# Layer 0's kept K page: first of its block instead of last, with the scores in a rotating PSUM bank

## The chip, the cores and the metric

The kernel runs on one core of one Trainium2 chip. The metric is the device time of one execution in microseconds (us). Three runs of the kernel before took 545.01 us in the median, 544.82 to 545.41. The profile shown is one more execution, taken with the hardware profiler.

## What is computed

A decode step with two layers, each of attention over a sliding window and of a gated feed-forward part. There is one query token of 640 numbers. Attention has 32 heads of 192 numbers, every head has its own K and V, and only the last 4096 positions of the cache are used. Both layers use the same weights and the same K and V caches:

```python
def _A_ref(x, k_cache, v_cache, wq, wo):
    ...
    k = jnp.repeat(k_cache[:, :, Sk - W:, :], rep, axis=1)      # W = 4096, rep = 1
    v = jnp.repeat(v_cache[:, :, Sk - W:, :], rep, axis=1)
    scores = jnp.einsum("bhqd,bhkd->bhqk", q, k) * (Dh ** -0.5)
    p = _softmax(scores, axis=-1)
    o = jnp.einsum("bhqk,bhkd->bhqd", p, v)
    ...

x = A_x
x = x + _A_ref(_layernorm(x, axis=-1), A_k_cache, A_v_cache, A_wq, A_wo)
x = x + _B_ref(_layernorm(x, axis=-1), B_w1, B_w3, B_w2)
x = x + _A_ref(_layernorm(x, axis=-1), A_k_cache, A_v_cache, A_wq, A_wo)
x = x + _B_ref(_layernorm(x, axis=-1), B_w1, B_w3, B_w2)
```

The layers must follow each other, but a K page read from memory for layer 0 can be used in layer 1 again if it stays on the chip.

## The kernel before

**Pages and slots.** Everything large is loaded in pages of 128 partitions x 6144 bf16 elements, 1536 KB: one page is the window of one head's K, or of its V, or a piece of a weight matrix. SBUF has an arena of 16 slots, one page each (`NSLOT`, L29). `loads` (L151-178) is the list of all pages in the order in which they are fetched. `refill` (L180) takes the head of that list whenever a slot is free and issues its DMA from the SP queue (L187); `done` (L203) gives a slot back and calls `refill`. This runs while the program is built, so which load takes which slot is fixed. On the chip, the load waits until the last reader of the slot's old page is over, and SP issues the loads strictly in the order of the list: a load whose slot is not free yet holds back those behind it.

**The loop.** `attention` (L429) goes over `i` from 0 to 41. Step `i` handles V page number `i - 10` (`LEAD`, L33) if there is one, and then K page number `i` if there is one. In this document K0 to K31 and V0 to V31 are these numbers, not head numbers. Heads come in blocks of eight (`HB`); `ORDER` (L146) gives the order of the blocks, 3, 2, 1, 0 in layer 0 and 1, 0, 2, 3 in layer 1. So K24 to K31 of layer 0 are heads 0 to 7. V0 to V7 belong to the first block, V24 to V31 to the last, and a block's V pages follow its K pages by ten steps. The loads stand in the same order: V(i - 10), K(i), V(i - 9), K(i + 1) and so on.

**A K page** (`k_page`, L272) is transposed in place by DVE in two halves (L281), then 12 matmuls on PE add the scores of its head into a PSUM bank that the eight heads of the block share. **The softmax of a block** (`softmax_head`, L294) runs after the eighth: a maximum over the bank, small transposes, the exponential on ACT (L310), one more transpose (L313). `softmax_place` (L316), two steps later, copies the probabilities into the tile `ptm` (five copies on ACT and three on DVE, L323) and takes the row sums with a matmul into `rl_ps` and a reciprocal (L327). **A V page** (`v_page`, L330) is 16 matmuls with `ptm` into the bank `o_ps` of its block; then its slot is given back. **`combine`** (L345) takes a finished block's o: ACT copies it out of PSUM (L347), two matmuls with `sel` bring it into `ot_ps`, and DVE scales and sums it (L353, L356). `rl_ps` and `ot_ps` are turns of the same single buffer in PSUM. In a block's first V step, the V page is done first and then the `combine` of the block before it (L440-444); the last block's `combine` stands after the loop (L462).

**What is kept for layer 1.** The K pages of 14 heads (`RETAIN`, L31) are not loaded again in layer 1. Thirteen of them simply keep their slot, already transposed. The fourteenth, head 7 (`STASH`, L30), gives its slot back: `stash` (L191) copies its page from SBUF to PSUM, five banks of 512 x 4 bytes a partition into the tile `pss`, and the rest of the page to the SBUF tile `rest` (L195, L198, all on DVE). In layer 1, in the place of head 7's load, the page is copied back into a free slot (L189). The closer layer 0 comes to its end, the more slots are held by kept pages; at its end three slots are left for all other pages.

**PSUM.** `pss` is five banks of the eight. In layer 0 the scores of block 0, 1, 2 and 3 use its banks 0, 1, 0 and 1 (L452). In layer 1 the first two blocks' scores come from the pool `ps_a` (L450), since `pss` still holds the kept page. `ps_a` is two banks in rotation, used by q, by the o of each block and by the projections. `ps_m` is one bank for small things.

So head 7, K31, is the last K page of layer 0, while its block's scores are in bank 1 of `pss`: `k_page` saves four banks and the rest (L290), then the softmax reads the scores, and the last bank is saved after it (L457); then the slot is given back (L458).

All instructions shown are kept in program order on their engine (`pin`, L70).

Of the kernel before, what the change touches and what calls it, by code (L numbers as in the profile page):

```python
# [18 lines left out]
H = 32  # L19
# [3 lines left out]
HB = 8  # L23
NB = H // HB
PGW = 6144
# [4 lines left out]
STASH = 7  # L30
RETAIN = (0, 1, 2, 3, 4, 5, 6, 7, 8, 11, 14, 18, 21, 24)  # L31
NSTASH = 5120
# [4 lines left out]
def _ap(t, p0, npart, off, dims):  # L37
    ps = t.ap[0][0]
    return bass.AP(t.tensor, t.offset + p0 * ps + off, [[ps, npart]] + [list(d) for d in dims])
# [3 lines left out]
def kernel(  # L43
# [13 lines left out]
    nc = tc.nc  # L57
# [12 lines left out]
    def pin(ins):  # L70
        tc.keep_in_program_order(ins)
        return ins

    def mm(*a, **k):
        return pin(nc.tensor.matmul(*a, **k))  # L75
# [57 lines left out]
    arena = arn.tile([P, NSLOT * PGW], BF16, name="arena")  # L133
# [14 lines left out]
    def head(layer, g):  # L148
        return HB * ORDER[layer][g // HB] + g % HB

    for layer in range(2):  # L151
        for c in range(NCH):
            loads.append((("q", layer, c), [(0, PGW, wq_v[c])]))
        for i in range(H + LEAD):
            for kind, g, cache in (("v", i - LEAD, A_v_cache), ("k", i, A_k_cache)):
                if not 0 <= g < H:
                    continue
                h = head(layer, g)
                if kind == "k" and layer == 1 and h in RETAIN:
                    if h == STASH:  # L160
                        loads.append((("k", 1, h), []))
                    continue
                loads.append(((kind, layer, h),
                              [(0, PGW, cache[0, h, S0:SK, :].rearrange("(p t) d -> p (t d)", p=P))]))
        for w in range(6):
            parts, ci, end = [], 9 * w, min(9 * w + 9, 48)
            while ci < end:
                to = min(end, ci - ci % 12 + 12)
                parts.append((640 * (ci - 9 * w), 640 * (to - ci),
                              wo_v[ORDER[layer][ci // 12]][:, 640 * (ci % 12):640 * (ci % 12 + to - ci)]))  # L170
                ci = to
            loads.append((("o", layer, w), parts))
        loads.append((("fa", layer), [(0, PGW, w1_v[:, 0:PGW])]))
        loads.append((("fb", layer), [(0, PGW, w3_v[:, 0:PGW])]))
        loads.append((("fc", layer), [(0, 1536, w1_v[:, PGW:]), (1536, 1536, w3_v[:, PGW:]),
                                      (3072, 2560, w2_v[:, 0:2560])]))
        loads.append((("fd", layer), [(0, 3840, w2_v[:, 2560:6400]), (3840, 640, w2_v[:, 6400:7040])]
                      + [(None, 640, w2_v[:, 7040:7680])] * (layer == 0)))

    def refill():  # L180
        while free and loads:
            key, parts = loads.pop(0)
            s = free.pop(0)
            home[key] = s
            for off, n, src in parts:
                dst = arena[:, s * PGW + off:s * PGW + off + n] if off is not None else keep[:]
                pin(nc.sync.dma_start(out=dst, in_=src))  # L187
            if not parts:
                stash(arena[:, s * PGW:s * PGW + PGW], False, range(5), True)  # L189

    def stash(x, save, banks, tail):  # L191
        xu, pu, ru = x.bitcast(U32), pss[:].bitcast(U32), rest[:].bitcast(U32)
        for k in banks:
            a, p = xu[:, 512 * k:512 * k + 512], pu[:, 512 * k:512 * k + 512]
            pin(nc.vector.tensor_copy(out=p if save else a, in_=a if save else p))  # L195
        if tail:
            a = xu[:, NSTASH // 2:PGW // 2]
            pin(nc.vector.tensor_copy(out=ru if save else a, in_=a if save else ru))  # L198

    def page(key):  # L200
        return arena[:, home[key] * PGW:home[key] * PGW + PGW]

    def done(key):  # L203
        free.append(home.pop(key))
        refill()
# [57 lines left out]
    def build_w(b):  # L263
        for a in range(4):
            dst = _ap(wst[:], 32 * a, 32, 8 * a + 7, [[382, 4], [191, 2], [32, 6]])
            src = _ap(qt_sb[:], 32 * a, 32, 4 * b, [[1, 4], [96, 2], [16, 6]])
            if a % 2 == 1:
                pin(nc.scalar.copy(out=dst, in_=src))  # L268
            else:
                pin(nc.gpsimd.tensor_copy(out=dst, in_=src))  # L270

    def k_page(layer, g, s_ps):  # L272
        h = head(layer, g)
        hl = h % HB
        fresh = layer == 0 or h not in RETAIN
        key = ("k", layer if fresh or h == STASH else 0, h)
        x = page(key)
        if fresh:
            w = PGW // KSPLIT
            for sp in range(KSPLIT):  # L280
                pin(nc.vector.transpose(x[:, w * sp:w * (sp + 1)].bitcast(U32), x[:, w * sp:w * (sp + 1)].bitcast(U32)))  # L281
        for it in range(6):
            be, par = divmod(it, 2)
            for th in range(2):
                mm(s_ps[32 * th:32 * th + 32, :], lhsT=wst[:, hl, it, :],
                   rhs=_ap(x, 0, P, 3072 * th + 64 * be + par, [[192, 16], [2, 32]]),
                   start=(hl == 0 and it == 0), stop=(hl == HB - 1 and it == 5),
                   tile_position=(0, 32 * th))
        if layer == 0 and h == STASH:
            stash(x, True, (0, 2, 3, 4), True)  # L290
        elif layer == 1 or h not in RETAIN:
            done(key)

# [51 lines left out]
    def combine(pos, o_ps, rl):  # L345
        o_sb = w20
        pin(nc.scalar.copy(out=o_sb[:, 0:384], in_=o_ps[:, 0:384]))  # L347
        ot_ps = ps_m.tile([P, 16, 12], F32, tag="m", name="ot_ps")
        for par in range(2):
            mm(ot_ps[:].rearrange("p q e -> p (q e)"), lhsT=sel[:, par, :, :].rearrange("p h q -> p (h q)"),  # L350
               rhs=o_sb[:, 192 * par:192 * par + 192], start=(par == 0), stop=(par == 1))
        om = w20[:, 384:576].rearrange("p (q e) -> p q e", q=16)
        pin(nc.vector.scalar_tensor_tensor(out=om, in0=ot_ps[:], scalar=rl[:], in1=mask[:].unsqueeze(2).broadcast_to([P, 16, 12]),  # L353
                                           op0=ALU.mult, op1=ALU.mult))
        with nc.allow_low_precision("one nonzero term in each sum"):
            pin(nc.vector.reduce_sum(out=otd[:, 12 * pos:12 * pos + 12], in_=om.rearrange("p q e -> p e q"),  # L356
                                     axis=AX.X))
# [71 lines left out]
    def attention(layer):  # L429
        layernorm()  # L430
        if layer == 0:
            flat = _ap(wst[:], 0, P, 0, [[1, wst[:].free_size()]])
            pin(nc.vector.memset(flat.bitcast(U32), 0))
        qproj(layer)
        s_ps, o_ps, soft, rl = {}, {}, {}, {}
        for i in range(H + LEAD):
            if i >= LEAD:
                g = i - LEAD
                b = g // HB
                if g % HB == 0:  # L440
                    o_ps[b] = ps_a.tile([P, 512], F32, tag="a", name="o_ps")
                v_page(layer, g, o_ps[b])
                if g % HB == 0 and b:
                    combine(b - 1, o_ps.pop(b - 1), rl.pop(b - 1))
            if i < H:
                b = i // HB
                if i % HB == 0:
                    build_w(ORDER[layer][b])
                    if layer == 1 and b < 2:
                        s_ps[b] = ps_a.tile([P, 512], F32, tag="a", name="s_ps")  # L450
                    else:
                        s_ps[b] = pss[:, 512 * (b % 2):512 * (b % 2) + 512]  # L452
                k_page(layer, i, s_ps[b])
                if i % HB == HB - 1:
                    soft[b] = softmax_head(b, s_ps.pop(b))
                    if layer == 0 and i == H - 1:
                        stash(page(("k", 0, STASH)), True, (1,), False)  # L457
                        done(("k", 0, STASH))  # L458
            if (i + 1 - LEAD) % HB == 0 and 0 <= (i + 1 - LEAD) < H:
                b = (i + 1 - LEAD) // HB  # L460
                rl[b] = softmax_place(b, *soft.pop(b))
        combine(NB - 1, o_ps.pop(NB - 1), rl.pop(NB - 1))  # L462
        wo_proj(layer)

    refill()
    ob = cst.tile([P, NCH], BF16, name="ob")
    for layer in range(2):
# [34 lines left out]
```

## Time and profile before

| | us |
|---|---|
| median of three runs | 545.01 |
| the profiled execution | 543.21 |
| its span, first to last instruction | 541.3 |
| PE busy | 286.6 (53%) |
| DVE busy | 225.7 (42%) |
| ACT busy | 41.9 (8%) |
| memory read | 222.40 MB, 411 GB/s over the span |

How to read it: the span is what the profiler saw, the time around it is 1.9 us. "Busy" is the time in which an engine has an instruction of its own in hand; PE's share includes matmuls that overlap. The page's second part cuts the span into 40 equal slices of 13.5 us and gives for each the busy tenths of the engines, the granted TensorE clock and the rate of the DMA. The chain of waits follows the work that ended last backwards from the end. Groups of instructions carry the line of the kernel; all matmuls carry L75, that of a helper, and are told apart by their tiles: `pss` and `s_ps` are scores, `o_ps` is V, `ot_ps` and `rl_ps` are the small ones of `combine` and `softmax_place`. A window lists busy time of each engine, the granted clock, the DMA share and the rate in one stretch. Where a line ends in brackets, they hold the engine's idle time before it and what ended it.

### The profile page before, as it was taken

The page shows a single profiled execution, that of the slowest core. Times are in us where ns is not written, and L with a number is a line of the kernel's source. Part 1 is how long each engine was busy: PE and PEld are TensorE (multiplying, and loading weights), DVE is VectorE, ACT ScalarE, POOL GpSimd, SP SyncE. Part 2 cuts the span into 40 slices and gives each one's busy share as a digit, 9 for nine tenths or more (in the row PEclk, how much of TensorE's full clock was granted, in tenths as well). Part 3 has the DMA queues.
Part 4 walks back from the last instruction along what each step waited for, and adds up shares of the span by engine and source line. Part 5 has one row for each costly group of instructions (what it writes and reads, how often), then busy time and mean ns, then how long its engine had stood idle before and what let it go on. Part 6 is the DMA issues. An engine that isn't in the chain of part 4 may idle for free.

```text
span 541.3 us, 5693 instructions
## 1 busy us (share of the span) xinstructions
PE 286.6 (53%) x2400; PEld 117.6 (22%) x2400; DVE 225.7 (42%) x271; ACT 41.9 (8%) x107; POOL 14.6 (3%) x52
## 2 busy tenths in 40 slices
PE   2355375555663655614445437684555655553544
PEld 1111132222221222201112212241222222221221
DVE  1189755575446654430001119516435644530011
ACT  1100200020001100020000000202000300020000
POOL 5100000000000000000000000000000000000000
PEclk9999765667567757755555658897886677565557
DMA  8999999999999999769999999999999999999995
GB/s 355 425 433 429 428 430 426 433 430 427 431 426 431 431 427 431 306 243 431 423 424 395 419 431 390 425 430 430 428 430 428 429 431 430 429 428 429 426 427 205
DMA packets 22633, 222.77 MB, mean 412 GB/s; under 512 B 2768, under 2 KB 3152, under 8 KB 5456
## 3 DMA queue, kind: packets, MB, share of 16 engines
q1 hardware_dynamic: 22464, 222.41, 97.2%
q8 instruction: 19, 0.31, 0.2%
q14 instruction: 6, 0.05, 0.0%
q10 hardware_dynamic: 144, 0.00, 0.0%
HBM read 222.40 MB, written 0.00 MB: 411 GB/s over the span
## 4 chain that ended last, share of the span: by engine, by line
DMA 78%; PE 11%; DVE 7%; issue 2%; ACT 1%; SPq 0%; POOL 0%; DVEq 0%; ACTq 0%; POOLq 0%
DMA arena<-in_A_k_cache_dram 49%; DMA arena<-in_A_v_cache_dram 10%; DMA arena<-in_A_wo_dram 7%; DMA arena<-in_A_wq_dram 7%; DMA arena<-in_B_w_dram 5%; DVE arena L281 4%; PE pss L75 3%; PE s_ps L75 3%; PE o_ps L75 3%; PE y_ps L75 1%; DVE pss L195 1%; PE q_ps L75 1%; PE u_ps L75 0%; SPq L187 0%; ACT w L310 0%
## 5 line engine op out<-in xcount | busy, mean ns | idle before, releaser
L281 DVE STREAM_TRANSPOSE arena<-arena 128x1536 uint32<-128x1536 uint32 x100 | 171.5, 1755 | 101.2 <-DMA arena<-in_A_k_cache_dram 97.1
L75 PE MATMUL pss<-arena,wst 128*32 128x512 bf16 x576 | 133.2, 545 | 133.7 <-DVE arena L281 131.0
L75 PE MATMUL o_ps<-arena,ptm 128*16 128x384 bf16 (+1 forms) x1024 | 126.5, 459 | 41.2 <-DMA arena<-in_A_v_cache_dram 38.1
L75 PEld LDWEIGHTS <-wst 128*32 128x32 bf16 x768 | 54.1, 114 | 235.5 <-issue 195.0
L75 PEld LDWEIGHTS <-ptm 128*16 128x16 bf16 (+2 forms) x1036 | 47.4, 106 | 82.7 <-issue 69.3
L75 PE MATMUL s_ps<-arena,wst 128*32 128x512 bf16 x192 | 27.5, 426 | 9.2 <-ACT wst L268 4.0
L353 DVE SCALAR_TENSOR_TENSOR w<-ot_ps,rl,mask 128x192 bf16<-128x192 f32 x8 | 3.3, 418 | 63.5 <-PE ot_ps L75 63.5
L75 PE MATMUL y_ps<-arena,otd 128*1 128x320 bf16 x192 | 17.2, 458 | 15.8 <-DMA arena<-in_A_wo_dram 15.8
L305 ACT ACTIVATE tb<-m 32x32 f32<-32x32 f32 x8 | 1.8, 228 | 301.6 <-DVE m L302 301.6
L75 PE MATMUL q_ps<-arena,xs 128*32 128x384 bf16 x160 | 14.5, 519 | 18.4 <-DMA arena<-in_A_wq_dram 15.8
L323 ACT COPY ptm<-w 32x128 bf16<-32x128 bf16 x40 | 16.1, 404 | 26.4 <-PE o_ps L75 24.1
L226 DVE CAST w<-y_ps 128x320 bf16<-128x320 f32 x4 | 2.0, 492 | 37.2 <-PE y_ps L75 37.2
L75 PEld LDWEIGHTS <-xs 128*32 128x32 bf16 x240 | 9.2, 125 | 37.2 <-issue 28.3
L251 DVE CAST ptm<-q_ps 128x768 bf16<-128x768 f32 x2 | 1.9, 958 | 31.4 <-ACT w L249 31.4
L270 POOL COPY wst<-qt_sb 32x48 bf16<-32x48 bf16 x16 | 6.2, 386 | 231.7 <-PE pss L75 190.8
L75 PEld LDWEIGHTS <-otd 128*1 128x1 bf16 x192 | 6.5, 102 | 26.4 <-issue 22.2
L295 DVE TENSOR_REDUCE t<-pss 64x1 f32<-64x512 f32 x6 | 4.1, 682 | 12.4 <-PE pss L75 12.4
L313 DVE STREAM_TRANSPOSE w<-w 64x512 bf16<-64x512 bf16 x8 | 5.6, 705 | 7.2 <-ACT w L310 7.2
L347 ACT CAST w<-o_ps 128x384 bf16<-128x384 f32 x8 | 3.8, 480 | 58.5 <-PE o_ps L75 57.0
L75 PE MATMUL st_ps<-xsq,onesD 128*128 128x12 f32 x8 | 2.3, 367 | 9.2 <-DVE xsq L208 9.2
L295 DVE TENSOR_REDUCE t<-s_ps 64x1 f32<-64x512 f32 x2 | 1.4, 684 | 13.5 <-PE s_ps L75 13.5
L268 ACT COPY wst<-qt_sb 32x48 bf16<-32x48 bf16 x16 | 6.4, 398 | 4.3 <-DVE qt_sb L259 3.9
(78 smaller groups left out, 97.0 us busy)
## 6 DMA issues: line engine op xcount, KB each, us to landing
arena<-in_A_v_cache_dram SPq DMA_DIRECT2D x64, 1536.0 KB, 29.2
arena<-in_A_k_cache_dram SPq DMA_DIRECT2D x50, 1536.0 KB, 29.2
arena<-in_A_wq_dram SPq DMA_DIRECT2D x10, 1536.0 KB, 10.2
arena<-in_A_wo_dram SPq DMA_DIRECT2D x6, 1440.0 KB, 15.7
arena<-in_B_w_dram SPq DMA_DIRECT2D x4, 1536.0 KB, 13.7
arena<-in_A_wo_dram SPq DMA_DIRECT2D x4, 960.0 KB, 16.8
arena<-in_A_wo_dram SPq DMA_DIRECT2D x6, 480.0 KB, 14.2
arena<-in_B_w_dram SPq DMA_DIRECT2D x2, 960.0 KB, 13.3
```

Source lines behind the costliest of these rows:

```text
L75: return pin(nc.tensor.matmul(*a, **k))
L195: pin(nc.vector.tensor_copy(out=p if save else a, in_=a if save else p))
L226: pin(nc.vector.tensor_copy(out=y_sb[:, 320:640], in_=y_ps[1][:, 0:320]))
L251: pin(nc.vector.tensor_copy(out=q_rep[par][:], in_=src))
L268: pin(nc.scalar.copy(out=dst, in_=src))
L270: pin(nc.gpsimd.tensor_copy(out=dst, in_=src))
L281: pin(nc.vector.transpose(x[:, w * sp:w * (sp + 1)].bitcast(U32), x[:, w * sp:w * (sp + 1)].bitcast(U32)))
L295: pin(nc.vector.reduce_max(out=t0[:, 0:1], in_=s_ps[0:64, :], axis=AX.X))
L313: pin(nc.vector.transpose(et[:], e[:]))
L323: pin((eng.copy if eng is nc.scalar else eng.tensor_copy)(out=dst, in_=src))
L347: pin(nc.scalar.copy(out=o_sb[:, 0:384], in_=o_ps[:, 0:384]))
L353: pin(nc.vector.scalar_tensor_tensor(out=om, in0=ot_ps[:], scalar=rl[:], in1=mask[:].unsqueeze(2).broadcast_to([P, 16, 12]), op0=ALU.mult, ...
```

## The change

A new function gives the head of a K page, used for the K loads and in `k_page`; V pages keep the old one. In layer 0's last block the heads of K24 to K31 are now 7, 0, 1, 2, 3, 4, 5, 6. The page of head 7 is saved whole in `k_page` and its slot is given back there. The scores of that block go to a bank of `ps_a`. The matmul flags that open and close the sum of a block go by position and no longer by head. In all blocks but the first, in both layers, `combine` of the block before now stands ahead of the next block's o tile and V page.

```diff
+    def k_head(layer, g):
+        h = head(layer, g)
+        if layer == 0 and h // HB == STASH // HB:
+            h = HB * (h // HB) + (h + HB - 1) % HB
+        return h
...
-                h = head(layer, g)
+                h = (k_head if kind == "k" else head)(layer, g)
...
-    def stash(x, save, banks, tail):
+                stash(arena[:, s * PGW:s * PGW + PGW], False)
+
+    def stash(x, save):
         xu, pu, ru = x.bitcast(U32), pss[:].bitcast(U32), rest[:].bitcast(U32)
-        for k in banks:
+        for k in range(NSTASH // 1024):
             a, p = xu[:, 512 * k:512 * k + 512], pu[:, 512 * k:512 * k + 512]
             pin(nc.vector.tensor_copy(out=p if save else a, in_=a if save else p))
-        if tail:
-            a = xu[:, NSTASH // 2:PGW // 2]
-            pin(nc.vector.tensor_copy(out=ru if save else a, in_=a if save else ru))
+        a = xu[:, NSTASH // 2:PGW // 2]
+        pin(nc.vector.tensor_copy(out=ru if save else a, in_=a if save else ru))
...
     def k_page(layer, g, s_ps):
-        h = head(layer, g)
+        h = k_head(layer, g)
...
-                   start=(hl == 0 and it == 0), stop=(hl == HB - 1 and it == 5),
+                   start=(g % HB == 0 and it == 0), stop=(g % HB == HB - 1 and it == 5),
                    tile_position=(0, 32 * th))
         if layer == 0 and h == STASH:
-            stash(x, True, (0, 2, 3, 4), True)
+            stash(x, True)
+            done(key)
...
                 b = g // HB
+                if g % HB == 0 and b:
+                    combine(b - 1, o_ps.pop(b - 1), rl.pop(b - 1))
                 if g % HB == 0:
                     o_ps[b] = ps_a.tile([P, 512], F32, tag="a", name="o_ps")
                 v_page(layer, g, o_ps[b])
-                if g % HB == 0 and b:
-                    combine(b - 1, o_ps.pop(b - 1), rl.pop(b - 1))
...
-                    if layer == 1 and b < 2:
+                    if (layer, b) in ((0, 3), (1, 0), (1, 1)):
                         s_ps[b] = ps_a.tile([P, 512], F32, tag="a", name="s_ps")
...
-                    if layer == 0 and i == H - 1:
-                        stash(page(("k", 0, STASH)), True, (1,), False)
-                        done(("k", 0, STASH))
```

More of the change, by code (lines that the diff above doesn't have):

```diff
@@ L188, in refill @@
             if not parts:
-                stash(arena[:, s * PGW:s * PGW + PGW], False, range(5), True)
-    def stash(x, save, banks, tail):
+                stash(arena[:, s * PGW:s * PGW + PGW], False)
+    def stash(x, save):
         xu, pu, ru = x.bitcast(U32), pss[:].bitcast(U32), rest[:].bitcast(U32)
-        for k in banks:
+        for k in range(NSTASH // 1024):
             a, p = xu[:, 512 * k:512 * k + 512], pu[:, 512 * k:512 * k + 512]
             pin(nc.vector.tensor_copy(out=p if save else a, in_=a if save else p))
-        if tail:
-            a = xu[:, NSTASH // 2:PGW // 2]
-            pin(nc.vector.tensor_copy(out=ru if save else a, in_=a if save else ru))
+        a = xu[:, NSTASH // 2:PGW // 2]
+        pin(nc.vector.tensor_copy(out=ru if save else a, in_=a if save else ru))
     def page(key):
```

## The prediction

> **What bounds the kernel now.** I read the page's slices first, then the chain of waits, then what the SP queue waited for, then windows around the one place where the slices break.
>
> ```profile
> span 541.3 us, 5693 instructions
> ...
> GB/s 355 425 433 429 428 430 426 433 430 427 431 426 431 431 427 431 306 243 431 423 424 395 419 431 390 425 430 430 428 430 428 429 431 430 429 428 429 426 427 205
> ...
> DMA 78%; PE 11%; DVE 7%; issue 2%; ACT 1%; SPq 0%; POOL 0%; DVEq 0%; ACTq 0%; POOLq 0%
> ```
>
> See that nearly every slice moves 425 to 433 GB/s and that the chain is 78% DMA: the time is the time to stream 222.40 MB, plus the holes in the stream. The largest hole is in slices 17 and 18 (306, 243), that is 216 to 244 us, at the end of layer 0's attention. The windows there (columns: window, length, busy time of PE, PEld, DVE, ACT and POOL, PEclk, DMA share, GB/s):
>
> ```profile
> 220.00:225.00 5.00, 1.82 (x12) 0.61 (x10) 3.44 (x2) 0.00 (x0) 0.00 (x0) 0.84 1.02 420
> 225.00:230.00 5.00, 3.44 (x41) 1.43 (x37) 3.06 (x6) 0.00 (x0) 0.00 (x0) 0.80 0.29 121
> 230.00:235.00 5.00, 0.58 (x2) 0.60 (x3) 3.76 (x13) 2.24 (x7) 0.00 (x0) 0.54 0.00 0
> 235.00:240.00 5.00, 0.00 (x0) 0.00 (x0) 0.23 (x2) 1.25 (x3) 0.00 (x0) 0.50 0.98 353
> ```
>
> Against 428 GB/s on either side, 225 to 240 us lacks 5 x (1 - 121/428) + 5 + 5 x (1 - 353/428) = 3.6 + 5.0 + 0.9 = 9.5 us of transfer. Who holds the queue is in SP's waits (total, times, longest) and in the chain through the hole (start, us, what):
>
> ```profile
> SPq L187 <- DVE pss L195: 13.3, 1, 13.3
> ```
>
> ```profile
> 226.84 0.71 DVE pss L195
> ...
> 229.72 0.33 DVE rest L198
> 230.04 0.60 DVE t L295
> ...
> 232.92 0.70 DVE w L313
> 233.63 0.60 DVE pss L195
> ...
> 234.28 6.40 DMA arena<-in_A_v_cache_dram
> ```
>
> The last K page of layer 0 (K31, head 7) is copied to PSUM in four bank copies and a tail, then the softmax of its block must finish because the fifth bank holds the scores, then the fifth copy runs; only then is its slot free. The next load in SP's order, the first V page of the last eight heads (V24), has that slot. SP takes its loads in order, so V25 and V26, whose slots are free, stand behind it.
>
> The size of the hole a second time, from the V pages on PE:
>
> ```profile
> 227.80 0.83 PE L75 MATMUL o_ps<-arena,ptm 128*16 128x384 bf16 x16 [0.19 <-DMA arena<-in_A_v_cache_dram]
> 232.94 0.58 PE L75 MATMUL rl_ps<-l,lsel 64*128 64x1 f32 x2 [4.32 <-ACT w L310]
> 240.72 1.47 PE L75 MATMUL o_ps<-arena,ptm 128*32 128x384 bf16 x16 [7.20 <-DMA arena<-in_A_v_cache_dram]
> ...
> 244.37 1.46 PE L75 MATMUL o_ps<-arena,ptm 128*16 128x384 bf16 x16 [1.75 <-DMA arena<-in_A_v_cache_dram]
> 248.02 1.46 PE L75 MATMUL o_ps<-arena,ptm 128*16 128x384 bf16 x16 [2.19 <-DMA arena<-in_A_v_cache_dram]
> ```
>
> V23 has landed at 227.8 and V24 lands at 240.7; pages land 3.65 us apart (244.37 to 248.02). Without the hole V24 lands at 227.80 + 3.65 = 231.45, so the hole costs 240.72 - 231.45 = **9.27 us**. A page issued into the empty queue took 6.40 us, hence a page must be issued 6.40 - 3.65 = 2.75 us before the page ahead lands, or the stream breaks. V24 met 234.28 against 227.80 - 2.75 = 225.05: 9.2 late, the same number.
>
> **What the change removes.** Head 7 becomes K24. In the changed order of instructions its five bank copies and its tail follow its transposes and stand ahead of K25's transposes on DVE; its slot goes to K29. Every later load of this stretch then takes a slot that is freed one V page earlier: K30 that of V16 (before V17), V21 that of V17, and so on to V24, which takes that of V21. V21's last matmul ends at 220.55 in the chain, so V24 can be issued at 220.6, 4.4 us before its deadline of 225.05. The 9.27 us hole at this place goes. What is late next, one page at a time, with landings 3.65 apart from 227.80:
>
> V25 takes V22's slot. V22's matmuls end at 227.6 (the row at 226.18, 1.43 long); deadline 231.45 - 2.75 = 228.7; slack 1.1. V26 takes V23's slot, 227.80 + 0.83 = 228.6; deadline 235.1 - 2.75 = 232.35. V27 takes V24's slot, and V24 needs the softmax. K31's scores end at 226.81, as before, and the softmax now starts there. Its chain on DVE and ACT took 3.59 us (230.04 to 233.63), so it ends at 230.4; the five ACT copies into ptm take 2.06 (232.5), the copy of o 0.48 (233.0), its two matmuls 0.50 (233.6, now ahead of V24), V24 itself 1.47 at the granted clock of 0.50: 235.1. Deadline for V27: 238.75 - 2.75 = 236.0; slack 0.9. V28 takes V25's slot: 235.1 + 1.5 = 236.6 against 239.65. From there the three slots turn as they do now, with 3 us of slack. So nothing opens a new hole, by about 1 us at two pages.
>
> **What it adds and moves.** The copies are the same six (0.695 and 0.418 us in their rows), 3.9 us together, but now between K24 and K25:
>
> ```profile
> 171.90 3.44 DVE L281 STREAM_TRANSPOSE arena<-arena 128x1536 uint32<-128x1536 uint32 x2
> ...
> 176.62 3.44 DVE L281 STREAM_TRANSPOSE arena<-arena 128x1536 uint32<-128x1536 uint32 x2 [1.28 <-DMA arena<-in_A_k_cache_dram]
> ...
> 191.25 3.44 DVE L281 STREAM_TRANSPOSE arena<-arena 128x1536 uint32<-128x1536 uint32 x2 [3.91 <-DMA arena<-in_A_k_cache_dram]
> ```
>
> K24's transposes end at 175.3, the copies at 179.25, K25 starts there instead of at 176.62: 2.6 us late. Behind K25 wait its matmuls, the softmax copies, V16 and K26; V16 ends near 186 instead of 182.7. What hides this is DVE's 3.9 us of idle time ahead of K27 (191.25) and the depth of the queue: K29, which waits for the copies, is issued at 179.3 (before: 179.41, behind V15), with a deadline near 199; K30, behind V16, near 186 (before: 191.44) with a deadline near 207. Cost 0. If that cover were gone it is at least the 2.6 us, at most the copies' 3.9. The copies wait for nothing else: the bank of the block before was last read by its exponential, done at 171.0.
>
> Block 3's scores go to a rotating bank, last used by o of block 0, copied out at 122; no wait. The bank adds one turn to the rotation, so o of block 2 now takes the bank of o of block 1 and must follow its copy: the six inner combines stand ahead of the V page. On PE the V page now waits for one ACT copy (0.48), two matmuls (0.50) and, since the row sums share one PSUM tile with them, one reciprocal (0.17). No row of before shows that wait. From below it is 0 or somewhat less, where the copy is ready and the combine merely changes places; from above 0.48 + 0.50 + 0.17 plus ACT's five copies ahead, 2.06, makes 3.2. I take 1.1, the copies being over by then at most places, and none of it on the path: at four of the six places the load behind that V page is issued some 29 us ahead of landing (the median in the issue table, so 26 ahead of the deadline), at V16 of layer 0 it is K30 with 20 to spare, and at V24 it is in the sum for V27 above, with 0.9 to spare. Cost 0; with the cover gone, 6 x 3.2 = 19.
>
> In layer 1 the loads wait for the same pages as now under other slot numbers, and the page comes back at the same point. Cost 0.
>
> **Sum.** The profiled execution took 543.21 (span 541.3, 1.9 around it): less 9.27 gives span 532.0 and 533.9. The runs' median is 545.01, 1.8 above the profiled one; the same 9.27 off gives 535.7.
>
> **A rule of the skill.** The windows beside the hole show 428 GB/s for one core. The Trainium skill, "DMA: Bandwidth & Descriptors", section "Specifications", gives about 358 GB/s from HBM to one core, and says further down that this side binds; a 1.57 MB page would then take 4.4 us, the hole would be worth 8.5, and the time 536.5. The trace's rate is measured and decides. The same page's section "Anatomy of one DMA" has a copy at 2.0 us plus bytes over 436 GB/s, 5.6 for a page where the row shows 6.40; by it the two thin slacks would be 0.75 wider and the sum the same.
>
> **Rivals.** (a) A shorter hole opens one page later, at V25 or V27, because V22 or the combine ahead of V24 ends later than I put it. For: slacks of 1.1 and 0.9. Against: all terms are rows, V24 at its slow clock. Its price: at most the upper end of the combine's wait once more, 3.2, less the slack of 0.9, so 2.3 and 538.0; about half of it is likelier: 537.0. (b) The change doesn't do what it says: SP's queue is held at another page just as long, because the real end of the hole is the softmax, not the slot. V27 would have to be issued at 236.0 + 9.3 = 245.3, ten us after my V24. Time 545.0. Against it: SP's own wait names the PSUM copy. (c) Slower: the V page behind each moved combine holds back its slot. Place: the six block boundaries; price: up to 3.2 each, 19.2 in all, so 545.0 + 19.2 - 9.3 = 555 at worst; it outweighs the gain from 9.27 / 6 = 1.55 us on the path at every boundary, which needs the loads there to miss their deadlines. Five of the six have 20 us or more, so I hold it unlikely.
>
> **Chances.** Forecast 0.77, (a) 0.14, (b) 0.05, (c) 0.04. The likeliest gives 535.7. Its own range is 534.6 to 536.8 (runs spread by 0.6; the two ways of sizing the hole differ by 0.2; up to 0.9 for a slack that is not there). Taking in most of (a) makes 534.6 to 538.2. Faster by over 0.2% (1.1 us, about what a measurement here can tell from no change): forecast and (a), 0.91; within it, (b), 0.05; slower, (c), 0.04.
>
> **What would show it.** Right: slices 17 and 18 at 425 or more; the 13.3 us wait of SP on the PSUM copies gone; the six copies in one row near 175; V24 consumed near 233.6 and V25 to V28 waiting for DMA 3.65 apart from 235.1; K27's transposes again at 191.25; the span 532. Wrong: DMA idle again between 227 and 245, then the page after it on PE tells whether V25 (228.7) or V27 (236.0) missed its deadline; or the stream thinning at 186 to 200 us, which would be the copies; or at a block boundary elsewhere, which would be the combines.

## The result, and the profile after

The changed kernel takes 536.59 us in the median of four runs (535.34 to 537.56), beside 544.91 for the kernel before. The ratio is 0.9846, 95% interval 0.9824 to 0.9868: 8.4 us less. The forecast was 535.7, in a range of 534.6 to 538.2. The profiled execution took 536.54, its span is 534.4 where the forecast had 532.0. Two more series of the same kernel gave ratios of 0.9836 and 0.9834, 8.9 and 9.0 us. Gains are given by these ratios, which are not quotients of the two medians: in the third series the medians lie 10.0 us apart where the ratio gives 9.0.

The page of the changed kernel, whole span and DMA rate by slice:

```profile
span 534.4 us, 5680 instructions
...
GB/s 347 429 430 429 432 426 430 428 431 431 426 432 426 433 427 430 430 418 432 421 415 418 428 373 407 425 428 431 432 426 429 428 433 428 428 429 430 428 421 153
```

Slices 17 and 18, 306 and 243 before, are now 430 and 418. Slice 24, at 307 to 321 us, is 373. The windows around both places (length, busy time of PE, PEld, DVE, ACT and POOL, PEclk, DMA share, GB/s):

```profile
225.00:240.00 15.00, 8.42 (x91) 3.56 (x88) 4.38 (x14) 3.48 (x9) 0.00 (x0) 0.61 0.99 415
...
310.00:330.00 20.00, 12.08 (x89) 4.76 (x89) 13.97 (x10) 1.59 (x3) 1.19 (x3) 0.74 0.92 375
```

225 to 240 us, where before moved 158 GB/s in the mean, moves 415. The second place was thin before the change too: there 319 to 339 us moves 403 GB/s, and the two other profiles of the changed kernel have 409 and 402 from 310 to 330. What SP waited for (total, times, longest):

```profile
SPq L193 <- PE o_ps L75: 46.6, 28, 6.2
...
SPq L193 <- DVE rest L203: 5.9, 1, 5.9
```

The 13.3 us on the PSUM copies are gone. One wait on the copies' tail is there instead, 5.9 us, in the new place, behind a queue that is full. The DVE rows of that place, and the V pages on PE at the end of the layer:

```profile
172.13 3.44 DVE L286 STREAM_TRANSPOSE arena<-arena 128x1536 uint32<-128x1536 uint32 x2
175.49 3.58 DVE L201 COPY pss<-arena 128x512 uint32<-128x512 uint32 x5
178.98 0.42 DVE L203 COPY rest<-arena 128x512 uint32<-128x512 uint32 x1
179.31 3.43 DVE L286 STREAM_TRANSPOSE arena<-arena 128x1536 uint32<-128x1536 uint32 x2
...
187.76 3.42 DVE L286 STREAM_TRANSPOSE arena<-arena 128x1536 uint32<-128x1536 uint32 x2
191.44 3.44 DVE L286 STREAM_TRANSPOSE arena<-arena 128x1536 uint32<-128x1536 uint32 x2 [0.26 <-DMA arena<-in_A_k_cache_dram]
```

```profile
227.99 1.02 PE L75 MATMUL o_ps<-arena,ptm 128*16 128x384 bf16 x16 [0.34 <-DMA arena<-in_A_v_cache_dram]
...
232.78 0.48 PE L75 MATMUL ot_ps<-w,sel 128*128 128x192 bf16 x2 [3.00 <-ACT w L353]
233.19 1.47 PE L75 MATMUL o_ps<-arena,ptm 128*32 128x384 bf16 x16
235.34 1.46 PE L75 MATMUL o_ps<-arena,ptm 128*16 128x384 bf16 x16 [0.69 <-DMA arena<-in_A_v_cache_dram]
238.97 1.46 PE L75 MATMUL o_ps<-arena,ptm 128*16 128x384 bf16 x16 [2.17 <-DMA arena<-in_A_v_cache_dram]
242.62 1.46 PE L75 MATMUL o_ps<-arena,ptm 128*16 128x384 bf16 x16 [2.19 <-DMA arena<-in_A_v_cache_dram]
```

The copies stand at 175.5, K25 starts at 179.3, and K27 at 191.4 waits for its DMA again: DVE is back in step, with 0.26 us to spare. V24 begins at 233.2, held by the combine and no longer by its page, and V25, V26 and V27 (235.34, 238.97, 242.62) wait for DMA 3.65 us apart. The forecast had 233.6 and 235.1.

Where the rest of the forecast went can be read from the landings of single loads in the trace. V31 lands at 257.21, 8.95 earlier than before; the last q page of layer 1 at 310.81, 9.20 earlier. The fourth K load of layer 1 (head 13) lands only 7.22 earlier, the second V page there 8.13, and from the fourth wo page of layer 1 to the last load it is 7.3. The span is 6.9 shorter: after the last landing it goes on for 5.6 us, before for 5.2.

### The profile page after: what moved, and what is told of

It reads as the page before. It is cut to its first block, busy times and chain, and to the rows that moved or that the text cites. A ratio compares the mean times of both kernels' runs of the same rounds, so it can differ in the third digit from the quotient of the medians.

```text
span 534.4 us, 5680 instructions
## 1 busy us (share of the span) xinstructions
PE 288.6 (54%) x2400; PEld 118.7 (22%) x2400; DVE 225.7 (42%) x271; ACT 41.8 (8%) x107; POOL 14.6 (3%) x52
## 4 chain that ended last, share of the span: by engine, by line
DMA 80%; PE 11%; DVE 6%; ACT 1%; issue 1%; POOL 0%; SPq 0%; DVEq 0%; ACTq 0%; POOLq 0%
DMA arena<-in_A_k_cache_dram 50%; DMA arena<-in_A_v_cache_dram 13%; DMA arena<-in_A_wo_dram 8%; DMA arena<-in_B_w_dram 5%; DVE arena L286 4%; PE s_ps L75 4%; DMA arena<-in_A_wq_dram 4%; PE pss L75 2%; PE o_ps L75 2%; DMA xb<-in_A_x_dram 1%; PE y_ps L75 1%; PE q_ps L75 1%; ACT w L316 0%; DVE t L301 0%; PE u_ps L75 0%
## 5 line engine op out<-in xcount | busy, mean ns | idle before, releaser
L75 PE MATMUL pss<-arena,wst 128*32 128x512 bf16 x480 | 108.3, 539 | 107.4 <-DVE arena L286 104.7
L75 PE MATMUL o_ps<-arena,ptm 128*16 128x384 bf16 (+1 forms) x1024 | 124.8, 458 | 29.3 <-DMA arena<-in_A_v_cache_dram 27.6
L75 PE MATMUL s_ps<-arena,wst 128*32 128x512 bf16 x288 | 54.7, 502 | 34.0 <-DVE arena L286 28.5
L75 PE MATMUL ot_ps<-w,sel 128*128 128x192 bf16 x16 | 3.4, 309 | 8.7 <-ACT w L353 7.9
## 6 DMA issues: line engine op xcount, KB each, us to landing
arena<-in_A_v_cache_dram SPq DMA_DIRECT2D x64, 1536.0 KB, 29.2
arena<-in_A_k_cache_dram SPq DMA_DIRECT2D x50, 1536.0 KB, 29.2
```

## The experiments

The theory: the hole in the stream was set by the time at which DVE finished the last PSUM copy, because the load of V24 had that page's slot and SP keeps its order. The rivals: the order of the heads or the bank as such, the moved combine, and, for what the forecast missed, the other slots.

| kernel | median us | kernel before, run beside it | ratio to before, 95% interval |
|---|---|---|---|
| changed kernel | 536.59 | 544.91 | 0.9846, 0.9824 to 0.9868 |
| changed kernel, again | 535.16 | 544.12 | 0.9836, 0.9804 to 0.9868 |
| only the combines moved | 543.24 | 544.12 | 0.9982, 0.9964 to 1.0000 |
| copies after the softmax | 544.38 | 544.12 | 1.0006, 0.9985 to 1.0028 |
| kept page last, whole copy at once | 537.71 | 544.12 | 0.9890, 0.9862 to 0.9918 |
| o copied three times before V24 | 537.08 | 544.41 | 0.9873, 0.9846 to 0.9900 |
| o copied nine times before V24 | 538.05 | 544.41 | 0.9885, 0.9853 to 0.9916 |
| PSUM copies three times | 535.18 | 544.41 | 0.9837, 0.9812 to 0.9862 |
| even wo pages | 534.97 | 544.41 | 0.9829, 0.9803 to 0.9855 |
| 13 heads kept | 536.49 | 544.60 | 0.9862, 0.9837 to 0.9887 |
| even wo pages, again | 533.25 | 544.60 | 0.9797, 0.9771 to 0.9822 |
| changed kernel, third time | 534.59 | 544.60 | 0.9834, 0.9807 to 0.9861 |

**The changed kernel again** (two series, no edit).

> The changed kernel once more, to see which of its two losses come back. My theory: the hole ahead of V24 is gone in every execution (V pages 3.65 us apart from V23 on), and the 0.9 us that the time lacks of the forecast 535.7 is lost at places the change does not touch: the fourth K load of layer 1 took 8.4 us from issue to landing in an almost empty queue where the same load took 6.4 before, and one wo page of layer 1 landed 0.95 us late. If those two are chance, the profiled execution here lands that K load in 6.4 to 8.4 us and the time lies anywhere from 535 to 537.5. Rival: they belong to the change (other slots), then both are here again with the same size.

> The changed kernel as the companion of the two: 535 to 536.6, V24 to V31 without a hole above 1 us, and the fourth K load of layer 1 again with a landing between 6.4 and 8.5 us after its issue.

Measured: 535.16 and 534.59, the second just under its forecast of 535 to 536.6. In both V24 lands within 3.9 us of V23. The fourth K load of layer 1 lands 7.3 and 8.9 us after its issue, the second above the 8.5 that was expected; in both it is late, by 0.9 and 2.5 us. Two kernels below that keep the old hole have it 0.9 and 0.2 late as well, so the change alone is not the reason. The late wo page of layer 1 came back in the second series only: its lead over before is 6.5 us there against 7.5 of V31 ahead of it, in the first 9.0 against 8.5. But V27 now lands 4.26 and 4.12 us behind V26, 0.6 and 0.5 late, which it did not in the first profile, so the first expectation's 3.65 us from V23 on did not hold. So the big hole is gone every time, and small ones come and go, at V25, V27 and that K load.

**Only the combines moved.**

```diff
+                if g % HB == 0 and b:
+                    combine(b - 1, o_ps.pop(b - 1), rl.pop(b - 1))
                 if g % HB == 0:
                     o_ps[b] = ps_a.tile([P, 512], F32, tag="a", name="o_ps")
                 v_page(layer, g, o_ps[b])
-                if g % HB == 0 and b:
-                    combine(b - 1, o_ps.pop(b - 1), rl.pop(b - 1))
```

> The kernel before with only the six combines moved ahead of the V page. My theory: the moved combine holds PE back by about 1 us at six places that the stream does not wait for, so 545.0, within 0.5, and SP still waits 13 us on the PSUM copies. Rival (the combine is what helps, or what costs): 2 us or more off 545 in either direction, 536 if it were the whole of the gain, 550 if each of the six cost its 1 us.

Measured: 543.24, ratio 0.9982, 0.9964 to 1.0000. The windows of this kernel at the old place:

```profile
225.00:230.00 5.00, 4.52 (x41) 1.70 (x37) 2.96 (x5) 0.00 (x0) 0.00 (x0) 0.55 0.32 134
230.00:235.00 5.00, 0.58 (x2) 0.50 (x2) 3.77 (x13) 2.18 (x6) 0.00 (x0) 0.79 0.00 0
```

The hole is there unchanged, and SP waits 13.0 us on the PSUM copies. The combine ahead of the V page is not the gain of 8 to 9 us, nor a cost that can be measured; the interval leaves room for a gain of up to 2 us.

**The copies after the softmax**, with head 7 first and the scores in the rotating bank as in the changed kernel.

```diff
         if layer == 0 and h == STASH:
-            stash(x, True)
-            done(key)
+            pass
...
                     soft[b] = softmax_head(b, s_ps.pop(b))
+                    if layer == 0 and i == H - 1:
+                        stash(page(("k", 0, STASH)), True)
+                        done(("k", 0, STASH))
```

> The changed kernel with head 7 still first in its block and the scores still in the rotating bank, but the six copies and the release of the slot after the softmax of the block, where the fifth copy stood before. My theory (the time of the last copy is the hole, not the order of the heads): the softmax ends at 230.4, six copies of 3.9 us end at 234.3, V24 is issued there as before, and the time is that of before, 545.0, within 1. Rival (the order of the heads or the bank brings the gain): 536.6.

Measured: 544.38, ratio 1.0006. The chain of this kernel through the hole:

```profile
229.93 0.70 DVE w L318
230.63 0.60 DVE pss L201
...
234.16 0.44 DVE rest L203
...
234.61 6.26 DMA arena<-in_A_v_cache_dram
```

The copies end at 234.6 and V24's load is issued there, 0.3 us from the forecast and from the kernel before (234.28). The order of the heads, the bank and the moved combines are worth nothing that can be measured as long as the copies end late; the gain hangs on the end of the copies.

**The kept page last, copied whole at once**: the changed kernel without the new order of heads.

```diff
     def k_head(layer, g):
         h = head(layer, g)
-        if layer == 0 and h // HB == STASH // HB:
-            h = HB * (h // HB) + (h + HB - 1) % HB
         return h
```

> The changed kernel with the old order of the heads: head 7 is the last K page again, but its scores are in the rotating bank, so all six copies run straight after its transposes and the slot is free before the softmax. My theory: transposes end at 224.0, copies at 227.9, V24 is issued at 228.0 against its deadline of 225.05, so a hole of 2.9 us stays: 2.9 above the changed kernel, 539.5, a gain of 5.4 to 6.4 over before. Rival (the softmax is the end of the hole, the slot is not): 545. Rival (the bank alone does everything): 536.6.

Measured: 537.71, ratio 0.9890, 6.0 us less than before and 2.6 more than the changed kernel measured beside it. Its chain:

```profile
220.72 3.44 DVE arena L284 x2
224.16 0.60 DVE pss L199
...
227.66 0.32 DVE rest L201
227.99 0.60 DVE t L299
```

The copies run from 224.16 to 227.98, and V24's load is issued at 228.05, 3.0 us past the deadline of the forecast; V24 lands 6.31 us behind V23 where 3.65 is full rate, a hole of 2.66. So two thirds of the gain come with the bank, which lets the copies run ahead of the softmax, and the last third with the order. The intervals of this kernel and of the changed one (0.9804 to 0.9868) just touch, so the last third rests on the 2.66 us in the trace.

**O copied three and nine times in the combine ahead of V24**, an artificial delay of PE.

```diff
-        pin(nc.scalar.copy(out=o_sb[:, 0:384], in_=o_ps[:, 0:384]))
+        for _ in range(3 if extra else 1):       # 9 in the second kernel
+            pin(nc.scalar.copy(out=o_sb[:, 0:384], in_=o_ps[:, 0:384]))
...
-                    combine(b - 1, o_ps.pop(b - 1), rl.pop(b - 1))
+                    combine(b - 1, o_ps.pop(b - 1), rl.pop(b - 1), extra=(layer == 0 and b == 3))
```

> The changed kernel with ACT's copy of o made three times in the one combine ahead of V24 (2 x 0.48 = 0.96 us more before PE can take V24). My theory (there is about 1 us of slack at V27, so a late V24 costs nothing up to there): V27, issued at 234.7 in the changed kernel's profile against a deadline of 238.95 - 2.75 = 236.2, is issued at 235.7; no more than 0.3 us lost, 536.6. Rival (the moved combine is on the path): 1 us lost, 537.6.

> The same with nine copies of o (8 x 0.48 = 3.84 us more). My theory: V27 is issued at 238.5, 2.3 us past its deadline of 236.2, so V27 lands about 2.3 us later behind V26 than the 3.65 of the others, and the time is 539. Rival (the combine is on the path with all of it): 540.4. Rival (the path does not run through V27 at all): 536.6.

Measured: 537.08 and 538.05; by the ratios 1.9 and 2.5 us more than the mean of the changed kernel's three series (0.9839). The V pages of the second kernel on PE:

```profile
237.60 3.37 PE L75 MATMUL o_ps<-arena,ptm 128*32 128x384 bf16 x48
245.31 1.46 PE L75 MATMUL o_ps<-arena,ptm 128*16 128x384 bf16 x16 [4.34 <-DMA arena<-in_A_v_cache_dram]
```

With nine copies V24, V25 and V26 run in one row at 237.6 and V27 waits 4.3 us: it lands 6.60 behind V26, a hole of 2.95, where the forecast of this run had 2.3. With three copies V27 is issued at 236.21, by my deadline 0.5 us in time, and still lands 4.50 behind V26, 0.85 late; V25, which this edit does not touch, lands 0.66 late. With nine copies V31 lands at 259.89, 2.0 to 2.7 us later than in the three profiles of the changed kernel: the path does run through V27, and the slack there is smaller than I had worked out. That the times are above the changed kernel is not certain, neither with three copies nor with nine: the intervals overlap with those of its three series.

**The PSUM copies three times.**

```diff
-            stash(x, True)
+            for _ in range(3):
+                stash(x, True)
             done(key)
```

> The changed kernel with the six PSUM copies of the kept page made three times in their new place (2 x 3.9 = 7.8 us more of DVE between K24 and K25). My theory (DVE's idle time ahead of later K pages and the depth of the queue cover the copies): K29 is issued near 187 against a deadline near 199, DVE catches up 3.8 us with each later K page and is in step again by K29; no time lost, 536.6 within 1, and no slice under 415 GB/s between 175 and 230 us. Rival (the copies' cover is thin): up to 7.8 lost, 544.

Measured: 535.18, ratio 0.9837, the same as the changed kernel. The windows and DVE in this kernel:

```profile
185.00:195.00 10.00, 5.22 (x32) 2.00 (x32) 6.75 (x11) 0.48 (x1) 0.00 (x0) 0.50 1.01 429
195.00:205.00 10.00, 6.78 (x65) 3.13 (x58) 10.00 (x7) 0.00 (x0) 0.00 (x0) 0.66 1.01 430
```

```profile
195.06 10.07 DVE L286 STREAM_TRANSPOSE arena<-arena 128x1536 uint32<-128x1536 uint32 x6
205.70 3.44 DVE L286 STREAM_TRANSPOSE arena<-arena 128x1536 uint32<-128x1536 uint32 x2 [0.56 <-DMA arena<-in_A_k_cache_dram]
```

7.8 us more on DVE: it runs without a pause through K26, K27 and K28 and waits for K29's DMA at 205.7, in step, as expected. The stream keeps 429 and 430 GB/s. The new place of the copies has cover for three times their length.

**Even wo pages**: six pages of 8 chunks instead of five of 9 and one of 3.

```diff
-            parts, ci, end = [], 9 * w, min(9 * w + 9, 48)
+            parts, ci, end = [], 8 * w, 8 * w + 8
...
-                parts.append((640 * (ci - 9 * w), 640 * (to - ci),
+                parts.append((640 * (ci - 8 * w), 640 * (to - ci),
...
-            for cc in range(min(9, 48 - 9 * w)):
-                ci = 9 * w + cc
+            for cc in range(8):
+                ci = 8 * w + cc
```

> The changed kernel with the wo matrix cut into six even pages (8 chunks each, 1280 KB) instead of five of 9 chunks and one of 3. In the profile of the changed kernel the second feed-forward page of layer 0 lands 4.9 us after the first, not 3.65, because with three slots the short wo page leaves too few bytes in the queue. If short pages with three slots make that hole, it goes, and the time is 1.3 us below the changed kernel, 535.3. If the hole has another reason, 536.6.

> The even wo pages once more, beside the changed kernel on the same chip: the second feed-forward page landed 3.63 us after the first, so that hole is gone, but the gain over V31 to that page was only 0.6 to 0.8 us. 0.7 us below the changed kernel of this call if that is what it brings; if the pages behind give it back, the same time.

Measured: 534.97 and 533.25, ratios 0.9829 and 0.9797. In the first profile the second feed-forward page lands 3.63 us behind the first, not 4.9. In the second profile it lands 4.82 behind, though it is issued 5.9 us ahead of the first page's landing, and with 13 heads kept below it lands 4.95 behind, issued 6.4 ahead. So neither the short wo page nor the number of slots is the reason for this hole. One coincidence stands in the traces: instructions are loaded in pieces of 16 KB by a queue of their own (`q8`), and in all eleven profiles in which this page lands 0.7 to 1.6 us late, such a load starts 2.0 to 3.4 us before its landing; in the two in which it is on time (nine copies of o, first even pages) it starts 3.8 and 1.0 us before. Whether that is the cause was not tried.

In the series that has both, the even pages are 1.3 us below the changed kernel in the median, but their intervals (0.9771 to 0.9822 and 0.9807 to 0.9861) overlap. It is the fastest of the kernels here and clearly below the kernel before; against the changed kernel the gain is likely and not shown, nor is its place.

**13 heads kept instead of 14.**

```diff
-RETAIN = (0, 1, 2, 3, 4, 5, 6, 7, 8, 11, 14, 18, 21, 24)
+RETAIN = (0, 1, 2, 3, 4, 5, 6, 7, 8, 11, 14, 18, 21)
```

> The changed kernel with 13 heads kept instead of 14 (head 24 is loaded again in layer 1): one page more to stream, 3.65 us, and four slots instead of three from the end of layer 0's attention to the start of layer 1's K pages. My theory (what the stream still loses there, and what varies from one execution to the next, comes from loads issued into an almost empty queue, because three slots turn over too late): in the profile V25 and V27 land 3.65 us behind the page ahead of them, the two feed-forward pages 3.65 apart, and the fourth K load of layer 1 no later than its place; from V31's landing to the second V page of layer 1 the changed kernel took 81.1 us where 20.75 pages at 3.65 are 75.7, so up to 5.4 comes back against 3.65 more: between 1.7 faster and 1.5 slower than the changed kernel, with less spread. Rival (the slots are not the limit there): 3.65 slower, 540.

Measured: 536.49, 1.9 us above the changed kernel measured beside it (1.5 by the ratios), at or just past the upper end of my range of 1.5 and short of the rival's 3.65. The runs lie closer together, as expected: 536.42 to 537.62, against 534.22 to 537.35. The windows of this kernel:

```profile
230.00:240.00 10.00, 4.29 (x52) 1.94 (x53) 2.45 (x7) 2.48 (x6) 0.00 (x0) 0.81 1.01 430
...
310.00:330.00 20.00, 13.72 (x105) 5.38 (x98) 17.52 (x12) 1.59 (x3) 1.19 (x3) 0.80 1.01 431
```

With a fourth slot both places run at 430 and 431 GB/s (the changed kernel's first profile: 415 and 375). V25 and V27 land 3.63 and 3.65 behind the page ahead, the fourth K load 3.65. From V31 to the second V page of layer 1 it takes 77.5 us, where the three profiles of the changed kernel took 81.2, 79.4 and 81.3. So the fourth slot does help at these places: by the profiles 1.9 to 3.8 us come back, by the medians 1.75 of the page's 3.65. The second feed-forward page, which I expected 3.65 behind the first, is late in spite of it (4.95). Three slots with one load less look like the better choice still, but the intervals (0.9807 to 0.9861 and 0.9837 to 0.9887) overlap.

## Why the prediction was right, point by point

**What bounds the kernel, and the size of the hole.** Right. With the copies late the time is that of before, with the copies early but after the last K page 2.7 us of hole are left, with the copies after the block's first K page none ahead of V24. The forecasts for these two, 545.0 and 539.5, came out at 544.4 and 537.7; the second was forecast on the scale of the slower first series, 2.9 above the changed kernel, and is 2.6 above it.

**What is late next.** Right in order and nearly in time: V24 on PE at 233.2 (233.6 forecast), V25's load issued at 227.70 (227.6), V26's at 229.06 (228.6), V27's at 234.70 (235.1).

**The added copies, the moved combines, layer 1.** Right that they cost nothing measurable. At V16 the combine's wait is in the trace: the row sums end at 186.0, the reciprocal follows, the two matmuls start at 186.29, V16 at 186.72, and K30's load is issued at 188.24 where I had 186, with 18 us still to its deadline. The DVE slack at K27 was 0.26 us in the first profile, not the 1.3 that 3.9 less 2.6 gives. There the last eleven score matmuls of K25 took 2.72 us at a granted clock of 0.50, where before took 1.51 at 1.00; the row sums, the combine and K26, which come behind them, are later by as much. In the other two profiles the slack was 0.27 and 1.38. One figure of the prediction is off without effect: a load with 29.2 us from issue to landing is 29.2 - 6.4 = 22.8 us ahead of its deadline and not 26.

**The sum.** 9.27 forecast, 8.4, 8.9 and 9.0 measured, 0.3 to 0.9 less. Each of the three intervals takes in 9.27 (the first reaches from 7.2 to 9.6 us), so the times alone do not show a shortfall. The traces show where some is lost: in the three profiles V31 lands 8.95, 8.55 and 8.31 us earlier than before, the last two with V25 or V27 late, and the fourth K load of layer 1 is late in each. What was mis-sized is the deadline, "a page must be issued 6.40 - 3.65 = 2.75 us before the page ahead lands". The 6.40 is from one load, and that load was issued in a pause in which the queue moved nothing for 7.8 us. The fourth K load of layer 1 is a direct test: with three slots every one of these kernels issues it 2.74 to 2.83 us before the landing ahead of it, that is just in time by my rule. It should land 3.65 behind each time. It landed so:

| kernel | landing behind the page ahead, us |
|---|---|
| before | 3.65 |
| copies after the softmax | 3.84 |
| only the combines moved | 4.53 |
| changed, three profiles | 5.64, 4.56, 6.14 |
| kept page last | 4.23 |
| o copied three, nine times | 4.05, 5.80 |
| PSUM copies three times | 4.21 |
| even wo pages, twice | 4.18, 4.36 |
| 13 kept (issued 9.4 us ahead) | 3.65 |

So 2.75 is the best case and nothing in it is spare. V25 (issued 3.3 to 4.0 us ahead) lost 0 to 0.9, V27 (3.3 to 4.5 ahead) lost 0 to 0.94 without the artificial delay of nine copies. My rival (a), a shorter hole one page later, is partly what happens: at 0 to 0.9 us, not at the 1.3 that I gave it, and at the start of layer 1 as well, which the prediction has at no cost. There it also shows in kernels that keep the old hole, so that only part of it counts against the change.

**How the empty queue differs.** A load's semaphore rises in 16 steps as it lands, and the trace has the time of each. The spread between the first and the last step, in us:

```
                           V23     V24     V31     landing of V24 after issue
before                     1.61    0.81    0.70    6.40
copies after the softmax   1.77    0.79    0.69    6.26
kept page last             1.18    0.69    0.78    6.14
changed, first profile     1.95    2.02    1.35    10.71 (behind V23)
changed, third profile     1.84    1.88    1.86    11.06 (behind V23)
```

After a pause in which the queue runs empty the 16 steps come close together, and in the changed kernel's stream without a pause they stay 1.3 to 2.1 us apart. A page is there when its slowest step is, so this spread may be why a load into a short queue lands later. The Trainium skill, "DMA: Bandwidth & Descriptors", section "Why a DMA increments its semaphore by 16 and not by 1", says that each of up to 16 DMA engines adds one when its own share has landed, and that they finish independently; the spread fits that. The fourth K load of layer 1 does not bear it out: the page ahead of it has a spread of 2.85 us in the kernel before, and the K load lands 3.65 behind; in the second and third profile of the changed kernel that spread is 2.19, smaller, and the K load lands 4.56 and 6.14 behind. So what makes a load into a short queue late by 0 to 2.5 us stays open.

The same page's limit of about 358 GB/s for one core, which its note under the bandwidth table gives for both cores of the domain streaming, is not what this core meets: with a fourth slot the 20 us from 310 on run at 431 GB/s. No run here has a second core at work. The copy time of 5.6 us in the prediction comes from a fit that its section gives for loads issued by GpSimd, and no load here was issued so; 6.40 less 5.6 is 0.8, not 0.75.

**Rivals (b) and (c)** did not happen: with the copies gone from V24's path no other hole of that size opened (the thinnest slice between the first and the last moves 373 GB/s), and the combines alone are at 0.9982.

## What to carry to other kernels

Where loads go through one queue in a fixed order into few slots, look for the load whose slot is freed last and ask what instruction frees it; one late slot stops all loads behind it, also those whose slots are free. Move the work that frees it to a place where the queue is deep: the same six copies cost 9 us at the end of the layer and nothing, even three times over, seven pages earlier. Give a load into a short queue more time than the best latency in the trace: the same load, issued 2.7 to 2.8 us ahead of the landing before it, took 6.4 to 8.9 us here.

## What was not expected of the hardware

The spread of a load's 16 completion steps: 0.7 to 0.9 us after an empty queue, 1.2 to 2.3 us from V23 to V31 in a stream that never stops, and later in the execution more, up to 3.4 us at the start of layer 1 and 4.8 us near its end. And how much single executions of one kernel differ: the changed kernel's runs reach from 533.49 to 537.56 us, their spans from 531.3 to 535.2. That the spread of the steps makes this difference is not shown.
